# Delta-rule attention and two feed-forward layers on one core: another order of the blocks' stages

## The chip, the cores and the metric

One core of one Trainium2 chip runs the whole kernel. The metric is the device time of one execution in microseconds (us); the median of several runs counts. The engines are PE (matrix products), DVE, ACT and POOL (elementwise work) and SP, which issues all DMAs in program order. DVE, ACT and POOL each work through their instructions in the order in which the program issues them.

## The reference, cut to what matters

```python
for t in range(S):                       # B, H, S, D = 4, 8, 768, 48
    y[t] = q[t] @ state
    state += beta[t] * outer(k_n[t], v[t] - k_n[t] @ state)
x = y as [3072 tokens, 384]
h = x @ w_in;  x = (h * tanh(softplus(h))) @ w_out          # d_ff = 2048
P = exp(x @ w_gate - max);  8 rounds: P /= row sums; P /= column sums; P *= N / E
out = sum over e of P[:, e] * (relu(x @ w1[e]) @ w2[e])     # E = 8, F = 1024
```

## The kernel before, in words

The sequence is cut into 6 blocks of 128 positions, 512 tokens each over the 4 batches. Phase 1 goes through the blocks in 6 windows. Window c runs the first feed-forward layer on block c (16 groups of 128 hidden columns, loop L1267: `m_first`, `m_a`, `m_c`, `m_second`), then the hidden sums become the next input (`x2_done`, L993), and then expert 0 (8 groups, loop L1301: `e_first`, `e_relu`, `y0_second`). Every product is made of three passes with a high and a low part of each operand, since PE's fast number format is short. Phase 2 (L1362) does experts 1 to 7 in 168 pairs of (expert, block, group of 256 columns): `first` (L478) makes the products of seven-product form into four banks, `evacuate` (L503) turns them into the hidden values, `second` (L1335) multiplies by the second weight, a pair later.

Attention is hidden under phase 1. A block's *products* (`st_g`, L734) are the key-key and query-key products of 64 positions, copied out of PSUM, scaled and causally masked (`causal`, L706, on POOL). Then the triangular system of 32 x 32 pieces is eliminated on DVE: `lane_in_ops` (L768) transposes the pieces into a lane layout, `elim_ops` (L776) are 60 small operations, `st_lane_out` (L798) transposes back. The block's *chain* follows: `st_m1`, `st_place`, `st_m2` (L802 to L847) complete the inverse, and `st_z`, `st_w`, `st_s`, `st_y` (L852 to L914) carry the state through the block, each needing the one before. `st_x1` (L916) turns the tokens over for the first layer.

What sets the order is written out by hand. `window(c)` (L1188) puts stages at 28 marks (s0 to s15, f1 to f4, s16 to s23) according to the table `PLACES` (L1179): the chain of block c+1, and norms, loads and products of block c+2. `fill` (L1012) and `tick` (L590) take elimination operations from a queue `eq` at a given number of microseconds per group. The start-up (L1034 to L1165) does block 0's products, elimination and chain and block 1's products before window 0. While PE waits there, `warm` and `run_warm` (L1019 to L1031) issue products into a bank that nobody reads, the fillers. Part of block 1's elimination runs on POOL (`elim1`, L1120), the values are scaled on POOL (`prep_v`, L699).

The first layer's weights come as 64-bit numbers. `begin_decode` (ACT) and three DVE operations (`queue_decode`, L177) make 32-bit numbers of a chunk, `convert` (L231) splits it into high and low part (ACT, POOL), fetches a later chunk and stores the result to DRAM, from where later windows reload it (L242). The sums of expert 0 (`y0_done`, L952) and the hidden sums (`x2_done`, L1002) are copied into one tile `xr` and stored at once. `logits` (L1004) makes the gate's products of a block in one bank.

The eight rounds of column and row sums are a list of steps `sinks` (L370). `sink_step` takes one: two per group in window 5's last groups, then in phase 2 two after each `evacuate` and two after each `second`. In phase 2's first expert, x_begin/x_split/x_store (L452 to L469) make the split sums of the next block in four pairs; `acc_load` (L1366) loads expert 0's sums of a block, and when the rounds are done they are scaled by the gate, two tiles of 128 tokens per pair (L1401 to L1407).

Of the kernel before, what the change touches and what calls it, by code (L numbers as in the profile page):

```python
# [22 lines left out]
NTOK = B * S  # L23
# [61 lines left out]
def delta_mish_sinkhorn_kernel(  # L85
# [144 lines left out]

    def convert():  # L231
# [20 lines left out]
        if ch in w_dram:  # L252
            nc.sync.dma_start(out=w_dram[ch], in_=w.bitcast(F32))
        n = order_of[i] + 2
        if n < len(firsts):
            if kind(firsts[n]) == "plain":
                fetch(firsts[n])

# [100 lines left out]
    def sink_round_end():  # L359
# [3 lines left out]
        nc.vector.tensor_scalar(out=cr, in0=ps, scalar1=1e-9, scalar2=None, op0=ALU.add)  # L363
        nc.vector.reciprocal(out=cr, in_=cr)
        nc.vector.tensor_scalar(out=cr, in0=cr, scalar1=float(NTOK) / E, scalar2=None, op0=ALU.mult)
# [161 lines left out]
    if True:  # L527
# [173 lines left out]


# [65 lines left out]
        def lane_in_ops(c):  # L768
# [5 lines left out]
            )  # L774

# [167 lines left out]
        y0ps = {}  # L943

# [7 lines left out]
        def y0_done(c):  # L952
# [6 lines left out]
            nc.sync.dma_start(out=y0_dram[c], in_=y)  # L959
# [33 lines left out]
        def x2_done(c):  # L993
# [8 lines left out]
            nc.sync.dma_start(out=x2_dram[c], in_=xr)  # L1002

        def logits(c):  # L1004
            ps = bank()[:, 0:4 * E].rearrange("p (t e) -> p t e", e=E)
            for t in range(4):
                for k in range(KD):
                    mm(ps[:, t, :], lhsT=xr[:, k, t * 128:(t + 1) * 128], rhs=wg_sb[:, k, :], start=(k == 0), stop=(k == KD - 1))
            vec.tensor_copy(lg[:, 4 * c:4 * c + 4, :], ps)
# [24 lines left out]
        with tc.manual_schedule():  # L1034
# [8 lines left out]
            for t in range(4):  # L1043
                load_part(0, t, 1)
            for t in range(4):
                load_kq(1, t)
            load_vt(0)
# [28 lines left out]
            for _, op in lane_in_ops(0):  # L1076
                op()
# [6 lines left out]
            for t in range(4):  # L1084
                prep_ss(1, t)
            prep_root(1)
# [3 lines left out]
            for t in range(4):  # L1090
                run_warm(512, *[lambda hf=hf: st_g(1, t, hf, False) for hf in range(2)])
            el(12)
            for op in root_ops(1) + norm_ops(1, ALL):
                el(1)
                op()
            for t in range(4):
                prep_mb(1, t, nc.gpsimd)
            for t in range(2):
                mask_p(0, t)
            for t in range(2):  # L1100
                prep_v(0, t)
                first_r(0, t)
            for t in range(4):
                mask_g(1, t, nc.gpsimd)
            for t in range(2, 4):
                prep_v(0, t)
                mask_p(0, t)
            for n in range(3):
                begin_decode(n)
            el(len(e0) - 16)  # L1110
# [4 lines left out]
            in1 = deque(op for _, op in lane_in_ops(1))  # L1115
            in1.popleft()()
            elim_eng = [nc.gpsimd]
            ops1 = deque(op for _, op in elim_ops(1, elim_eng))

            def elim1(n, eng):  # L1120
                elim_eng[0] = eng
                for _ in range(min(n, len(ops1))):
                    ops1.popleft()()

            run_warm(2048, lambda: st_m1(0, 0), lambda: st_m1(0, 1))
            st_place(0, 0, (0, 2))
            while in1:
                in1.popleft()()
            run_warm(2048, lambda: st_m2(0, 0))

            def step(pool, decode, make, dve):
                elim1(pool, nc.gpsimd)
                decodes(decode)
                elim1(dve, nc.vector)
                converts(make)

            step(8, 1, 0, 0)
# [333 lines left out]
```

## Time and profile before

| | |
|---|---|
| median of 3 runs | 2372.87 us (2372.09 to 2378.44) |
| the profiled execution's own time | 2370.12 us |
| its span, first to last instruction | 2368.3 us |
| PE busy | 2254.5 us, 95% |
| DVE, ACT, POOL busy | 1236.1, 619.7, 529.4 us |
| DMA | 297 MB, 36% of 16 engines' span |

Times in rows are microseconds from the span's start unless ns stands with them. A row of a view of groups gives line, engine, operation, output and input names, shapes and count, then busy time and the mean of one in ns, then the idle time before them and what ended it. PE's clock is given as the granted share of 2.4 GHz: 1.0 is 2.4 and 0.5 is 1.2 GHz.

### The profile page before, as it was taken

The page shows a single profiled execution, that of the slowest core. Times are in us where ns is not written, and L with a number is a line of the kernel's source. Part 1 is how long each engine was busy: PE and PEld are TensorE (multiplying, and loading weights), DVE is VectorE, ACT ScalarE, POOL GpSimd, SP SyncE. Part 2 cuts the span into 40 slices and gives each one's busy share as a digit, 9 for nine tenths or more (in the row PEclk, how much of TensorE's full clock was granted, in tenths as well). Part 3 has the DMA queues.
Part 4 walks back from the last instruction along what each step waited for, and adds up shares of the span by engine and source line. Part 5 has one row for each costly group of instructions (what it writes and reads, how often), then busy time and mean ns, then how long its engine had stood idle before and what let it go on. Part 6 is the DMA issues. An engine that isn't in the chain of part 4 may idle for free.

```text
span 2368.3 us, 41965 instructions
## 1 busy us (share of the span) xinstructions
PE 2254.5 (95%) x18012; PEld 2084.9 (88%) x18012; DVE 1236.1 (52%) x2009; ACT 619.7 (26%) x1012; POOL 529.4 (22%) x439
## 2 busy tenths in 40 slices
PE   6698899999999999897999999999999999999998
PEld 3477778888888878897999999999999999999998
DVE  8875725427172123764555555555555555555554
ACT  5244332333323232221321221121122122112111
POOL 5586441331412051131300020030020002002000
PEclk7799999999999999998999999999999999999999
DMA  5367643637344565332231232222213113221321
GB/s 173 114 208 219 206 150 130 207 121 241 132 151 164 173 230 195 121 105 109 108 143 45 81 134 81 80 86 89 81 67 145 47 77 133 81 80 68 107 84 51
DMA packets 74441, 297.04 MB, mean 125 GB/s; under 512 B 7504, under 2 KB 39504, under 8 KB 68880
## 3 DMA queue, kind: packets, MB, share of 16 engines
q1 hardware_dynamic: 74256, 294.36, 36.0%
q8 instruction: 142, 2.33, 0.4%
q14 instruction: 43, 0.35, 0.0%
HBM read 247.15 MB, written 47.19 MB: 124 GB/s over the span
## 4 chain that ended last, share of the span: by engine, by line
issue 35%; PE 10%; DMA 5%; POOL 4%; DVE 1%; SPq 0%; ACT 0%; POOLq 0%; DVEq 0%; ACTq 0%
PE o L1348 5%; PE b L487 5%; DMA gr<-in_w_dram 4%; POOL gw L439 2%; POOL gx L439 1%; DMA acc<-y0d 1%; SPq L412 0%; POOL gx L466 0%; DVE acc L1353 0%; ACT gh L514 0%; DVE gt L510 0%; DVE gt L513 0%; ACT gw L437 0%; DVE gt L511 0%; DVE acc L1407 0%
## 5 line engine op out<-in xcount | busy, mean ns | idle before, releaser
L487 PE MATMUL b<-gx,gw 128*128 128x256 f32 x3564 | 452.5, 284 | 17.7 <-DVE gt L510 12.4
L487 PEld LDWEIGHTS b<-gx,gw 128*128 128x128 f32 x3564 | 444.2, 192 | 22.5 <-DVE gt L510 14.1
L1348 PE MATMUL o<-gw,gh 128*128 128x384 f32 x1728 | 443.0, 337 | 2.1 <-DVE acc L1353 2.1
L514 ACT ACTIVATE gh<-gt 128x1024 fp32r<-128x1024 f32 x168 | 178.3, 1061 | 647.2 <-DVE gt L513 647.2
L1348 PEld LDWEIGHTS o<-gw,gh 128*128 128x128 f32 x1728 | 309.7, 190 | 2.6 <-issue 2.6
L296 PE MATMUL psh<-xh,w 128*128 128x512 f32 x864 | 289.0, 416 | 23.2 <-DMA w<-wd 12.9
L515 DVE SCALAR_TENSOR_TENSOR gl<-gt,gh 128x1024 fp32r<-128x1024 f32 x168 | 209.6, 1247 | 189.4 <-ACT gh L514 189.4
L1348 PE MATMUL o<-gw,gl 128*128 128x384 f32 x864 | 291.1, 337 | 0.0
L510 DVE TENSOR_TENSOR gt<-b,gt 128x512 f32<-128x512 f32 x168 | 116.2, 691 | 302.0 <-PE b L487 238.1
L1348 PE MATMUL o<-gx,gh 128*128 128x384 f32 x960 | 247.5, 339 | 2.4 <-DVE acc L1353 2.4
L487 PE MATMUL b<-gx,gx 128*128 128x256 f32 x1980 | 243.7, 280 | 0.8 <-ACT gt L509 0.6
L487 PEld LDWEIGHTS b<-gx,gx 128*128 128x128 f32 x1980 | 240.4, 188 | 2.2 <-ACT gt L509 1.2
L296 PEld LDWEIGHTS psh<-xh,w 128*128 128x128 f32 x864 | 160.8, 195 | 65.1 <-issue 19.1
L978 POOL TENSOR_TENSOR gl<-x,gh 128x512 fp32r<-128x512 f32 x96 | 128.7, 1340 | 394.1 <-ACT gh L977 393.8
L439 POOL TENSOR_TENSOR gw<-gr,gw 128x512 fp32r<-128x512 f32 x72 | 90.8, 1293 | 561.4 <-ACT gw L437 561.4
L296 PE MATMUL psh<-xl,w 128*128 128x512 f32 x432 | 176.0, 407 | 4.2 <-DVE xl L607 4.2
L1348 PEld LDWEIGHTS o<-gx,gh 128*128 128x128 f32 x960 | 171.6, 188 | 2.9 <-issue 2.0
L1348 PEld LDWEIGHTS o<-gw,gl 128*128 128x128 f32 x864 | 163.6, 189 | 0.4
L1348 PE MATMUL o<-gx,gl 128*128 128x384 f32 x480 | 162.7, 339 | 0.0
L509 ACT ACTIVATE gt<-b 128x256 f32<-128x256 f32 x168 | 64.2, 382 | 352.2 <-PE b L487 328.9
L989 PE MATMUL x<-gh,w 128*128 128x512 f32 x576 | 150.0, 396 | 0.0
L439 POOL TENSOR_TENSOR gx<-gr,gx 128x512 fp32r<-128x512 f32 x40 | 50.4, 1294 | 440.9 <-ACT gx L437 440.9
(182 smaller groups left out, 2992.2 us busy)
## 6 DMA issues: line engine op xcount, KB each, us to landing
w<-wd SPq DMA_DIRECT2D x120, 768.0 KB, 4.6
gx<-xcd SPq DMA_DIRECT2D x36, 2304.0 KB, 9.0
gr<-in_w_dram SPq DMA_DIRECT2D x56, 384.0 KB, 3.6
wd<-w SPq DMA_DIRECT2D x24, 768.0 KB, 4.7
xcd<-gx SPq DMA_DIRECT2D x6, 2304.0 KB, 11.0
kq<-in_qkb_dram SPq DMA_DIRECT2D x20, 256.0 KB, 7.0
vt<-in_vtok_dram SPq DMA_DIRECT2D x6, 768.0 KB, 8.3
kq<-in_w_in_dram SPq DMA_DIRECT2D x12, 384.0 KB, 4.7
```

Of the source, the lines that this page charges most:

```text
L296: mm(ps, lhsT=wi(u, pw, kc), rhs=(xh, xl)[px][:, kc, :], start=(n == 0), stop=(n == 3 * KD - 1))
L439: nc.gpsimd.tensor_tensor(out=w[:, 1, q:q + 512], in0=r[:, q:q + 512], in1=w[:, 0, q:q + 512].bitcast(F32), op=ALU.subtract)
L487: mm(ps, lhsT=w[:, pw, a * 128:a * 128 + 128], rhs=x[:, px, b, :], start=(n == 0), stop=(n == last))
L509: nc.scalar.activation(out=t[:, 7], in_=b0[:, 0], func=AF.Copy)
L510: tt(out=t[:, 0:7:6], in0=b1, in1=t[:, 7:8].to_broadcast([128, 2, 256]), op=ALU.add)
L514: nc.scalar.activation(out=h, in_=t[:, 0:4], func=AF.Relu)
L515: nc.vector.scalar_tensor_tensor(out=l, in0=t[:, 0:4], scalar=0.0, in1=h.bitcast(F32), op0=ALU.max, op1=ALU.subtract)
L978: nc.gpsimd.tensor_tensor(out=l, in0=p, in1=h.bitcast(F32), op=ALU.subtract)
L989: mm(x2ps[c][k], lhsT=wo(u, pw, k * 128, k * 128 + 128), rhs=(h, l)[pg], start=(f == 0 and n == 0), stop=(f == U1 - 1 and n == 2))
L1348: mm(o[t], lhsT=(h, l)[ph][:, z, (t % 2) * 128:(t % 2) * 128 + 128], rhs=w[:, pw, at:at + DM], start=(g == 0 and fi == 0 and n == 0), stop ...
```

## The change

- Start-up: nearly all fillers go. Block 1's elimination leaves the start-up; `lane_in_one` and `elim_ops` of block 1 go into the queue `eq` for window 0. Its root goes from ACT and DVE to POOL's `prep_pow`, its norms and masks come later. The lane of blocks 0 and 1 is taken in by one transpose, after ACT copies (`diag_left`) and followed by POOL clearing (`diag_clear`). Block 0's values are scaled by 32 ACT operations (`prep_v_act`), its causal masks stand after the elimination in program order. Its value load is issued ahead of block 1's product operands. Four chunks instead of six are decoded before window 0, five and not six begun.
- `PLACES`: block 1's chain starts at mark 13 of window 0, two stages per mark, and block 2's products move from window 0 to marks 0 to 3 of window 1; block 3's products and block 2's chain are in window 1, block 4's with block 3's chain in window 2, and so on.
- Stores: a weight chunk's store is issued after the next chunk's fetch (`late_stores`); the stores of `xr` come three groups (expert 0's sums) or one group (hidden sums) later (`late_xr`).
- The gate's products are made in four parts, each copied out a mark later.
- In window 5 and in phase 2 the sum steps stand before the group's first products, two per pair (four in pair 0). Token sums are scaled four tiles per pair. `x_store(0)` goes from window 5 to pair 1, x_begin and x_split go one pair later. Two operations of a round's end become one.

The diff, cut:

```diff
@@ convert
-        if ch in w_dram:
-            nc.sync.dma_start(out=w_dram[ch], in_=w.bitcast(F32))
         n = order_of[i] + 2
         if n < len(firsts):
             if kind(firsts[n]) == "plain":
                 fetch(firsts[n])
+        flush_stores()
+        if ch in w_dram:
+            late_stores.append(lambda: nc.sync.dma_start(out=w_dram[ch], in_=w.bitcast(F32)))
@@ new
+        def prep_v_act(c, t):
+            ne = nrms[c % 2][1]
+            for h in range(H):
+                x = vt(c)[:, t, h * D:h * D + D]
+                nc.scalar.activation(out=x, in_=x, func=AF.Copy, scale=ne[:, t * H + h:t * H + h + 1])
+        def diag_left(c, t):
+            g = gx(c)[:, t]
+            for p in (32, 96):
+                nc.scalar.activation(out=g[p:p + 32, :, 0:32], in_=g[p:p + 32, :, 32:64], func=AF.Copy)
+        def lane_in_one(c):
+            v = gx(c).rearrange("p t h x -> p x (t h)")
+            return [
+                (1.94, lambda: nc.vector.transpose(out=lane, in_=v[:, 0:32, :])),
...
+                (0.0, lambda: diag_clear(c)),
@@ start-up
-            for _, op in lane_in_ops(0):
+                diag_left(0, t)
+            for _, op in lane_in_one(0):
                 op()
...
+                prep_v_act(0, t)
+            for t in range(4):
+                prep_ss(1, t)
+            prep_pow(1, ALL)
...
-            run_warm(2048, lambda: st_m1(0, 0), lambda: st_m1(0, 1))
+            work(1, 0)
+            run(lambda: st_m1(0, 0), lambda: st_m1(0, 1))
             st_place(0, 0, (0, 2))
...
+            for op in norm_ops(1, ALL):
+                op()
+            for t in range(4):
+                prep_mb(1, t, nc.gpsimd)
+            warm(1)
+            run(lambda: st_w(0, 0), lambda: st_w(0, 1))
+            work(2, 1)
...
+            for t in range(4):
+                diag_left(1, t)
+            eq.extend(lane_in_one(1) + elim_ops(1))
@@ PLACES
+            (13, two(17, 18, 20, 21, 22, 23, 24, 25), []),
+            (11, two(14, 15, 17, 18, 20, 21, 23, 24), [
+                (2, None, [-1, -1, 0, 1], two(0, 1, 2, 3), None, 3),
+                (3, 1, [14, 15, 17, 20], two(16, 19, 22, 25), 1, 25),
+            ]),
+            (5, spread(8, 23, 1, 16), [(4, 1, [9, 10, 12, 14], spread(11, 24, 1, 8), 1, 19)]),
+            (1, spread(4, 19, 1, 16), [(5, 1, [5, 6, 8, 10], spread(7, 19, 1, 8), 1, 19)]),
+            (0, spread(3, 19, 1, 16), []),
+            (0, [], []),
@@ windows
-                rate(0.4 if c == 0 else 0.6)
+                rate(0.6)
...
+                    if f == 4:
+                        flush_xr()
...
-                    fill(2.0)
+                    fill(2.0 if c else 1.7)
@@ phase 2
+                sink_step()
+                sink_step()
                 first(p)
                 evacuate(p)
-                sink_step()
-                sink_step()
+                if p == 0:
+                    sink_step()
+                    sink_step()
             if p >= 1:
                 second(p - 1)
-                sink_step()
-                sink_step()
...
+                if p == 1:
+                    x_store(0)
                 if e == 1 and i + 1 < NBLK:
-                    if g == 0:
+                    if g == 1:
                         x_begin(i + 1)
...
             if not sinks and todo:
-                for _ in range(2):
+                for _ in range(4):
```

## Rows read from the trace of the kernel before

**Rows 1.** Page: busy us, share of span and count; granted clock in 40 slices.

```profile
PE 2254.5 (95%) x18012; PEld 2084.9 (88%) x18012; DVE 1236.1 (52%) x2009; ACT 619.7 (26%) x1012; POOL 529.4 (22%) x439
...
PEclk7799999999999999998999999999999999999999
```

**Rows 2.** By stretch: length; busy PE, PEld, DVE, ACT, POOL; clock, DMA, GB/s.

```profile
0.00:113.81 113.81, 77.20 (x1126) 49.72 (x1126) 96.97 (x149) 44.36 (x133) 62.17 (x66) 0.73 0.45 138
113.81:275.19 161.38, 143.97 (x1441) 119.26 (x1441) 104.89 (x141) 66.71 (x110) 111.48 (x89) 0.93 0.66 218
275.19:425.41 150.22, 140.31 (x1392) 117.30 (x1389) 73.58 (x157) 44.23 (x82) 45.50 (x41) 0.94 0.48 159
425.41:565.34 139.93, 136.84 (x1392) 113.82 (x1390) 62.33 (x128) 43.78 (x82) 44.93 (x41) 0.99 0.53 172
565.34:704.00 138.66, 135.02 (x1392) 112.49 (x1390) 62.37 (x128) 43.79 (x82) 44.95 (x41) 1.00 0.49 162
704.00:830.48 126.48, 125.99 (x1200) 104.95 (x1198) 29.26 (x44) 36.36 (x62) 20.53 (x16) 1.00 0.48 163
830.48:950.19 119.71, 113.09 (x507) 93.85 (x505) 34.45 (x80) 39.02 (x61) 40.99 (x31) 0.94 0.54 205
```

**Rows 3.** Groups of DVE, 22 to 62.3: elimination of block 0.

```profile
L790 DVE TENSOR_TENSOR lane<-lane,t 128x30 f32<-128x30 f32 (+14 forms) x30 | 18.1, 603 | 0.9
L784 DVE TENSOR_TENSOR t<-lane 128x30 f32<-128x30 f32 (+14 forms) x30 | 18.0, 599 | 0.9
```

**Rows 4.** Groups of DVE, 660 to 800: elimination of a later block.

```profile
L790 DVE TENSOR_TENSOR lane<-lane,t 128x30 f32<-128x30 f32 (+14 forms) x30 | 10.0, 332 | 1.0
L784 DVE TENSOR_TENSOR t<-lane 128x30 f32<-128x30 f32 (+14 forms) x30 | 9.9, 331 | 0.9
```

**Rows 5.** Timeline of POOL: start us, us, operation, names, shapes, count, idle before.

```profile
35.34 5.58 POOL L709 TENSOR_TENSOR kq<-kq,mask_sb 64x512 f32<-64x512 f32 x4
...
221.24 5.45 POOL L656 TENSOR_TENSOR ne<-ss,half_sb 128x32 f32<-128x32 f32 x1 [6.87 <-DVE ss L640]
```

**Rows 6.** By stretch, columns as in rows 2: start-up, window 1, phase 2.

```profile
62.20:113.81 51.61, 37.63 (x694) 26.02 (x694) 45.74 (x55) 14.29 (x22) 31.81 (x35) 0.74 0.32 106
...
367.64:387.55 19.91, 17.35 (x231) 14.42 (x229) 9.47 (x15) 5.14 (x10) 5.89 (x7) 0.85 0.36 129
954.28:983.33 29.05, 22.55 (x124) 21.73 (x123) 21.06 (x50) 7.30 (x9) 8.66 (x6) 0.82 0.23 73
1067.41:1083.84 16.43, 9.83 (x58) 9.63 (x58) 9.32 (x19) 1.44 (x2) 0.00 (x0) 0.79 0.27 112
...
1083.84:1091.96 8.12, 8.12 (x59) 8.12 (x58) 5.18 (x9) 3.35 (x5) 2.15 (x1) 1.00 0.00 0
```

**Rows 7.** Timeline of DVE, start-up.

```profile
19.76 3.87 DVE L772 STREAM_TRANSPOSE lane<-gx 32x1024 f32<-32x1024 f32 x2
...
117.97 1.89 DVE L607 TENSOR_TENSOR xl<-psa,xh 128x512 fp32r<-128x512 f32 x3
```

**Rows 8.** Timeline of ACT, start-up.

```profile
13.68 0.24 ACT L650 ACTIVATE sq<-kt 128x48 f32<-128x48 f32 x1 [5.05 <-DMA kt<-in_ktok_dram]
...
13.92 0.23 ACT L650 ACTIVATE sq<-kt 128x48 f32<-128x48 f32 x1
...
22.69 4.86 ACT L704 ACTIVATE kq<-psa 64x512 f32<-64x512 f32 x8
...
37.44 0.76 ACT L704 ACTIVATE kq<-psa 64x256 f32<-64x256 f32 x2
...
113.16 1.57 ACT L922 ACTIVATE xh<-psa 128x512 fp32r<-128x512 f32 x3 [2.50 <-POOL w L249]
```

**Rows 9.** Timeline of PE, window 1.

```profile
296.71 1.19 PE L296 MATMUL psh<-xh,w 128*128 128x512 f32 x2 [6.84 <-DMA w<-wd]
```

**Rows 10.** Chain of waits, 1050 to 1085: start us, us, what.

```profile
1060.53 12.57 DMA acc<-y0d
```

**Rows 11.** Waits: engine and line, waited for: us in total, times, longest us.

```profile
DVE acc L1407 <- DMA acc<-y0d: 32.8, 3, 15.2
```

More of the change, by code (lines that the diff above doesn't have):

```diff
@@ L229, in drain_elim, with flush_stores @@
             eq.popleft()[1]()
+    late_stores = deque()
+    def flush_stores():
+        while late_stores:
+            late_stores.popleft()()
     def convert():
@@ L943, in delta_mish_sinkhorn_kernel, with flush_xr @@
         y0ps = {}
+        late_xr = deque()
+        def flush_xr():
+            while late_xr:
+                late_xr.popleft()()
         def y0_second(u):
@@ L1001, in x2_done, with logits, logits_out @@
                     nc.scalar.activation(out=xr[:, k, :], in_=x2ps[c][k], func=AF.Copy)
[L1002 to L1009, printed above, removed]
+            late_xr.append(lambda: nc.sync.dma_start(out=x2_dram[c], in_=xr))
+        lgps = []
+        def logits(c, t):
+            ps = bank()[:, 0:E]
+            for k in range(KD):
+                mm(ps, lhsT=xr[:, k, t * 128:(t + 1) * 128], rhs=wg_sb[:, k, :], start=(k == 0), stop=(k == KD - 1))
+            lgps.append((lg[:, 4 * c + t, :], ps))
+        def logits_out():
+            nc.vector.tensor_copy(*lgps.pop(0))
         def fill(us):
@@ L1143, in delta_mish_sinkhorn_kernel, with work @@
-            run_warm(1024, lambda: st_y(0, 0), lambda: st_y(0, 1))
+            for t in range(4):
+                mask_p(0, t)
+            def work(decode, make):
+                decodes(decode)
+                converts(make)
+            work(1, 0)
+            run(lambda: st_m1(0, 0), lambda: st_m1(0, 1))
+            st_place(0, 0, (0, 2))
+            run(lambda: st_m2(0, 0))
+            st_place(0, 1, (0, 2))
+            run(lambda: st_m2(0, 1))
+            for op in norm_ops(1, ALL):
+                op()
@@ L1150, in delta_mish_sinkhorn_kernel @@
-            run_warm(512, lambda: st_w(0, 2), lambda: st_w(0, 3))
-            begins(6)
-            step(2, 5, 3, 0)
-            run_warm(512, lambda: st_y(0, 2), lambda: st_y(0, 3))
+            converts(2)
+            warm(2)
+            run(lambda: st_z(0, 2), lambda: st_z(0, 3))
+            work(3, 2)
+            warm(1)
+            run(lambda: st_w(0, 2), lambda: st_w(0, 3))
+            for t in range(4):
+                mask_g(1, t, nc.gpsimd)
+            work(4, 3)
+            warm(1)
@@ L1154, in delta_mish_sinkhorn_kernel @@
+            run(lambda: st_y(0, 2), lambda: st_y(0, 3))
             for n in range(6, 8):
                 fetch(n)
-            step(4, 6, 5, 6)
             converts(4)
+            begins(5)
             early_ctx.close()
@@ L1165, in delta_mish_sinkhorn_kernel @@
             warm(2)
+            for t in range(4):
+                diag_left(1, t)
+            eq.extend(lane_in_one(1) + elim_ops(1))
         NU = U1 + U2
@@ L1192, in window @@
             late = {m: [] for m in MARKS}
-            nxt, far = c + 1, c + 2
-            rest[f"s{U1 + (c < NBLK - 1)}"].append(lambda: logits(c))
+            nxt = c + 1
+            for t in range(4):
+                k = MARKS.index(f"s{U1}") + (1 + t if c < NBLK - 1 else t // 2 - 1)
+                rest[MARKS[k]].append(lambda t=t: logits(c, t))
+                rest[MARKS[k + 1]].append(logits_out)
             if c == 0:
@@ L1275, in delta_mish_sinkhorn_kernel @@
                         m_c(b + f - 1)
-                    if not c and f < m0:
-                        elim1(10, nc.gpsimd)
                     if f == 0 and c:
```

146 lines of the change are left out of this document (61 added, 85 removed).

## The prediction, made before any run of the change

> **What bounds the kernel now.** I read the profile's page first: PE is busy 95% of the span, and the clock row is at its upper level except near the start and around the middle [rows 1]. So the time to win is where PE waits or runs at 1.2 GHz. The table by stretch [rows 2] cuts the span at the first weight product of each window of phase 1 and at the first one of phase 2. The start-up before window 0 takes 113.8 us at a mean clock of 0.73. Window 0 takes 161.4, window 1 150.2, window 2 139.9, window 3 138.7, window 4 126.5, window 5 up to phase 2 119.7. Windows 2 and 3 carry one block's chain and another block's products, window 4 a chain alone: a block's products cost some 12.2, the difference of windows 3 and 4. Against that, window 0 is about 23 too long and window 1 about 11.
>
> Inside the start-up the engine that decides is DVE. Its elimination of block 0 is 60 small operations. They take 0.60 us each there [rows 3], and 0.33 in a later block where POOL is quiet [rows 4]; 36.1 us against 19.9. POOL was at its causal masks meanwhile, 1.4 us each [rows 5]: a DVE operation with both operands in SBUF then lasts about as long as the POOL one. From 62.2 to 113.8 DVE is busy 45.7 of 51.6 [rows 6]. The first product of window 0 waits for the tokens' low part, which DVE ends at 119.9 [rows 7].
>
> **The change, part by part.** *Start-up, first half.* One transpose of 128 partitions takes in the lane, so two smaller ones, 3.87 together, go [rows 7]; ACT copies put ahead of it (two of 256 elements at 0.38 [rows 8] are on the path) cost 0.9 with their waits. Elimination starts 3 us earlier, at 20.8. With POOL quiet it takes 19.9 + 1.8 of idle [rows 4]. POOL's power of the norms now lands beside it: 5.45 [rows 5]. No row shows it beside a DVE operation on SBUF, so it costs between 0 and 5.45; I take 5, since the masks of the same engine did hold DVE up. The eight norm operations of block 1 leave this stretch. Elimination ends near 47.5, with two transposes of 2 us at 51.5; before it was 62.3 and 66.2.
>
> What is late next is ACT, which works in order. After its copies of the query products (end 27.5), it scales the values in 32 small operations (at most 0.24 each by the squares, which have a read-out between them [rows 8]; 0.19 taken, 6 us), then squares block 1 (32 at 0.24, 7.5), makes 24 copies of block 1's products at 0.38 (9.1), two negations (1) and four scalings of 768 (an estimate of 0.8 from 0.52 for 512, 3.2): 54.3. The first chain product's copies stand behind all this. So this point moves from 66.2 to 54.3: 12 us.
>
> *Start-up, second half.* From there to the end of the low parts it was 53.7. DVE loses a lane transpose set (5.9), 14 elimination operations of block 1 (4.6 at 0.33, 8.4 at 0.6; 7), and two of six decodes (six operations, some 1.4 each beside POOL; 8), and gains four norm operations (1). That is 20 off the engine that decides, for 34 us. POOL loses 18 or so elimination steps but gets block 1's masks, before the conversion that the token copies wait for [rows 8]; that is why I take no more. The low parts end near 88.5 and not 119.9, and the second group of window 0 starts 30.5 earlier. Bounds: 20, if ACT is 10 later than summed, to 36, if the power costs nothing.
>
> The fillers go with it. They ran in PE's waiting time, so I cost their removal at nothing; what it costs if they kept the clock up is next. With them the clock was still 0.73 in the mean before window 0 [rows 2]. The Trainium skill, page "TensorE: Matmul & The Clock Gate", section "Why this matters for your kernels", advises against idle gaps between bursts of products because the clock falls back. By that rule the chain's products would all run at the lower level. I estimate them at 20 of PE's 37.6 us from 62.2 on, the rest being fillers [rows 6]; from a mean clock of 0.74 to 0.5 they take 10 more. I keep the sum as it is, as DVE and ACT, not PE, end last there.
>
> *Window 0.* Block 2's products leave it: -12.2, with the wait for that block's loads, 0 to 6, taken as 5. DVE gets block 1's elimination in it: about 54 more operations and a transpose, while POOL has 89 instructions of 1.25 in the window [rows 2]. At 0.33 that is 18, partly in DVE's idle time (104.9 busy of 161.4); if every POOL instruction of the first 14 groups shut DVE out, it would be 25. I take 12, between the two. Sum -5.
>
> The Trainium skill, page "SBUF — State Buffer", section "Who interferes with whom", calls the port that DVE and GpSimd share an exclusive lock held for a whole instruction. By a strict reading window 0 would be 13 worse than summed; the rows show one DVE operation done per POOL mask, so not quite that. It is the first rival below.
>
> *Window 1* gets block 2's products: +12.2. The wait of 6.84 for a reloaded weight [rows 9] should go: SP issues in order, and the store of token sums, which waited for copies out of PSUM, no longer stands ahead of the reloads: -7. The chain no longer bunches in the group before the hidden sums, 19.9 long [rows 6], where two ordinary groups and the sums take about 13: -7. Sum -2.
>
> *Windows 2 to 4*: the stores' place, the gate logits in four pieces, and the norm's power away from a chain step; 0 to 4 each, taken as 5 in all. *Window 5*: the sums' products stand ahead of the weight products: -2. Late weight stores, one fused operation in each of eight rounds: nothing, DVE has room there. The first block's split sums are stored after pair 1, in a queue with room.
>
> *Phase 2.* The pairs from 954.3 to 983.3 take 29.05 where two take 2 x 8.12 [rows 6]: PE waits with the column sums' product, queued behind a pair. In the new order that product's input is made a pair earlier: -11, leaving 2. But the token sums are now scaled four per pair and not two. They catch up with their loads at the end of block 1 already, in pairs 7, 11 and 15. There DVE waits in order for a load that is 12.57 under way [rows 10], with the next evacuation behind it; before, it waited three times for 32.8 in all [rows 11], and two of them cost PE 16.4 - 8.1 = 8.3 each [rows 6]. A third such: +7. Sum -4.
>
> **The sum**: -30.5 - 5 - 2 - 5 - 2 - 4 = -48.5, on a profiled execution of 2370.1: 2321.6. The median of the runs is 2.75 above that execution, so I predict 2324.
>
> **The rivals.** *A. The shared port takes it back.* Block 1's elimination and the decodes meet all of POOL's work in window 0, and the masks meet the decodes in the start-up. Price: 25 instead of 12 there, 8 in the start-up: 2345. For it: DVE was busy 97 of 113.8 and slowed threefold [rows 2, 3]. Against: DVE idles a third of window 0. The Trainium skill's page "SBUF — State Buffer", in the section named above, has this as its rule.
>
> *B. Slower: the clock.* Without fillers PE enters window 0 at 1.2 GHz, and DVE's pace leaves a hole in each group, so the clock does not rise. Window 0's products, some 126 us at the upper level (as in window 4, which holds as much [rows 2]), would take up to 126 more; the holes of about 2 us in each of 24 groups, and DVE's share of the groups, hide half of that: 60 more, 2384. It decides from 48 us on, that is if more than three quarters of window 0 stay at the lower level. Against: window 0 had holes before and a mean clock of 0.93 [rows 2]. The Trainium skill's page "TensorE: Matmul & The Clock Gate", in the section named above, points this way.
>
> *C. Only the start-up counts.* The later windows keep their waits, because reloads are held by PE's use of the slots and not by SP: 7 in window 1, 5 in windows 2 to 4 and 2 in window 5 are lost: 2338.
>
> *D. The change does not do what it says*: ACT's 27 us of work before the first chain product grows, or a load of the first weights is late, so that the start-up gains 10 and not 30.5, and window 0 nothing: 2350.
>
> **How the numbers follow.** The forecast has 0.70, A 0.10, B 0.05, C 0.08, D 0.07. The forecast's own bounds (start-up 20 to 36, window 0 -18 to +8, the rest -22 to -5) reach from 2298 to 2345 with not all ends at once; A, C and D end at 2350, and 2356 allows for A with D in part. Range 2298 to 2356; left out are B, and a little on either side. A measurement of this kernel can tell about 0.3%, 7 us, from no change. Faster by more: the forecast, A and C, and nearly all of D, 0.93; within it 0.03; slower 0.04, most of B.
>
> **What would show it.** In the changed profile: elimination of block 0 at 0.33 to 0.45 per operation and done before 50; ACT without idle time from 20 to 54; the first weight product of window 0 near 87 and its group 4 to 5 long; window 0 about 150 to 155 with DVE and POOL both near full in its first half; window 1 near 148 without a wait for a reloaded weight; the first three pairs of phase 2 without the wait for the column sums; three waits of the evacuation for a token sum's load. The prediction is wrong if the weight products of window 0 start after 100, if window 0 takes over 170, or if the clock is under 0.8 in it.

## The result, and the profile after

The changed kernel takes 2402.43 us (median of 4 runs, 2397.57 to 2404.59), the kernel before on the same chip 2373.41: a ratio of 1.0115 [1.0094, 1.0137], so 27 us slower. Forecast were 2324 and a range up to 2356. The page, first the busy times and the clock, then the two groups of PE with the most idle time ahead of them:

```profile
PE 2261.3 (94%) x17981; PEld 2097.8 (87%) x17981; DVE 1255.1 (52%) x2057; ACT 632.8 (26%) x1059; POOL 500.1 (21%) x394
...
PEclk7898999999999999999999999999999999999999
...
L495 PE MATMUL b<-gx,gw 128*128 128x256 f32 x3564 | 460.3, 287 | 30.0 <-DVE gt L518 23.5
...
L305 PE MATMUL psh<-xh,w 128*128 128x512 f32 x864 | 290.4, 416 | 34.1 <-ACT x L1008 23.2
```

The same stretches as in [rows 2], with the same columns, cut at the first weight product of each window and of phase 2; the last row is phase 2 as a whole:

```profile
0.00:90.92 90.92, 70.40 (x1095) 50.94 (x1095) 66.40 (x126) 52.92 (x170) 43.02 (x34) 0.74 0.54 163
90.92:278.37 187.45, 147.56 (x1345) 118.91 (x1345) 127.67 (x163) 66.53 (x107) 89.19 (x58) 0.91 0.58 195
278.37:435.96 157.59, 146.26 (x1487) 123.31 (x1485) 86.45 (x162) 48.93 (x96) 58.97 (x59) 0.96 0.45 149
435.96:584.95 148.99, 138.48 (x1391) 115.63 (x1389) 79.80 (x171) 44.08 (x82) 45.02 (x41) 0.97 0.49 160
584.95:721.90 136.95, 134.54 (x1391) 112.39 (x1390) 61.56 (x131) 43.97 (x82) 44.75 (x41) 1.00 0.52 165
721.90:847.79 125.89, 125.66 (x1199) 104.83 (x1198) 29.45 (x47) 36.32 (x62) 20.54 (x16) 1.00 0.49 164
847.79:968.33 120.54, 112.65 (x506) 95.12 (x505) 30.49 (x71) 39.14 (x61) 40.86 (x31) 0.94 0.50 185
968.33:2402.80 1434.47, 1385.76 (x9587) 1376.68 (x9585) 773.29 (x1188) 300.89 (x402) 157.78 (x115) 0.99 0.26 93
```

Subtract [rows 2] line by line. The start-up is 22.9 shorter. Window 0 is 26.1 longer, window 1 7.4, window 2 9.1, window 5 0.8; windows 3 and 4 are 2.3 shorter. Phase 2 was 2368.30 - 950.19 = 1418.1 and is 16.4 longer. The sum is +34.5, the difference of the two spans. So the start-up gave nearly what it should, and window 0, windows 1 and 2, and phase 2 took it back with more.

**Window 0.** Counted from one group's first weight product to the next one's (s0 is the first group), s0 is 5.7 shorter than before, s3 to s13 are 9.7 longer (82.1 against 72.4), and s14 and s15, the last two groups before the hidden sums, are 22.0 longer (37.0 against 15.0). Expert 0's part is as long as it was, 58.0. In s14 and s15 block 1's `st_m1`, `st_m2` and the first stages of its chain now stand; before, then after, with the columns of [rows 2]:

```profile
202.21:217.20 14.99, 14.76 (x122) 11.92 (x118) 2.66 (x6) 6.27 (x12) 7.75 (x6) 1.00 0.82 257
183.38:220.40 37.02, 29.05 (x503) 24.30 (x502) 22.80 (x26) 16.95 (x28) 21.61 (x13) 0.80 0.57 168
```

PE has 503 products in them and not 122, and the clock is at 0.80 and not 1.00.

The groups before them show another cause. One of them, s6, 7.2 long where an undisturbed one takes 4.1, on DVE, then POOL, then ACT, then PE (timelines: start us, us, operation; in brackets the idle time before and its releaser):

```profile
122.63 1.94 DVE L816 TENSOR_TENSOR t<-lane 128x238 f32<-128x238 f32 x1
124.49 1.64 DVE L185 TENSOR_SCALAR kq<-kq 128x768 int32<-128x768 int32 x1
126.23 1.40 DVE L188 SCALAR_TENSOR_TENSOR kq<-kq 128x768 int32<-128x768 int32 x1
127.66 0.96 DVE L193 SCALAR_TENSOR_TENSOR kq<-kq 128x768 int32<-128x768 int32 x1
```

```profile
122.42 1.88 POOL L257 TENSOR_TENSOR w<-kq,w 128x768 fp32r<-128x768 f32 x1 [3.48 <-ACT w L256]
124.39 1.30 POOL L1015 TENSOR_TENSOR gl<-x,gh 128x512 fp32r<-128x512 f32 x1
125.67 1.14 POOL L703 TENSOR_TENSOR vt<-vt,ne 128x384 f32<-128x384 f32 x1
```

```profile
128.65 0.92 ACT L256 ACTIVATE w<-kq 128x768 fp32r<-128x768 f32 x1 [4.39 <-DVE kq L193]
...
130.26 0.58 ACT L1008 ACTIVATE x<-psh 128x512 f32<-128x512 f32 x1
```

```profile
130.89 0.50 PE L305 MATMUL psh<-xh,w 128*128 128x512 f32 x1 [1.03 <-ACT x L1008]
```

Read it from the end. PE waits for the activation L1008 to empty a bank. ACT works in order and has that activation behind the conversion L256, which waited 4.39 for DVE's decode. DVE had the decode behind elimination operations. And each DVE operation that meets one of POOL's three instructions ends shortly after that one does, 0.27, 0.44 and 0.82 later: L816, 0.41 where POOL is quiet (experiment 1), lasts 1.94 beside the 1.88 of L257. The wait of 1.03 is a third of the 3.1 that this group is too long. Most of the rest is the clock: after the wait ahead of the group, 1.93, it is at 0.57 in the group's first 4 us, and the nine weight products take 3.98 where those of s3 took 2.04 at 1.00:

```profile
123.65:127.63 3.98, 3.90 (x9) 2.81 (x10) 3.87 (x3) 0.61 (x1) 3.06 (x3) 0.57 0.53 126
```

DVE has no room left in these groups; the stretch from 101 to 185.5, columns as above:

```profile
101.32:185.50 84.18, 58.64 (x207) 42.06 (x206) 81.08 (x92) 30.02 (x43) 49.08 (x31) 0.92 0.58 192
```

**Phase 2.** In pair 0, whose first products begin at 968.33, PE stands 6.4 ahead of a sum's product, and DVE's timeline says why: evacuation first (971.46 to 976.3), then a whole round (from L372 on):

```profile
979.05 0.57 PE L370 MATMUL psa<-gate 128*128 128x8 f32 x2 [6.39 <-DVE gate L366]
```

```profile
971.46 0.68 DVE L518 TENSOR_TENSOR gt<-b,gt 128x512 f32<-128x512 f32 x1
...
976.25 0.16 DVE L372 TENSOR_SCALAR gate<-psa 128x8 f32<-128x8 f32 x1
...
978.41 0.49 DVE L366 TENSOR_REDUCE gate<-lg 128x8 f32<-128x192 f32 x1
```

By pairs, after less before: pairs 0 to 4 are +7.0, -5.2, -5.1, +1.2, +3.3 (+1.2 together), pair 9 is +9.1, and pairs 13 and 17 are +2.4 and +3.5. Pair 9 is the new wait for a token sum's load, its row first, then the waits for these loads, which were 32.8 [rows 11]:

```profile
1054.43:1071.61 17.18, 10.12 (x59) 9.91 (x58) 9.36 (x17) 2.36 (x3) 0.00 (x0) 0.80 0.23 98
```

```profile
DVE acc L1463 <- DMA acc<-y0d: 47.2, 3, 16.3
```

### The profile page after: what moved, and what is told of

The parts are those of the page before. It is cut to its first block, busy times and chain, and to the rows that moved or that the text cites. A ratio compares the mean times of both kernels' runs of the same rounds, so it can differ in the third digit from the quotient of the medians.

```text
span 2402.8 us, 41937 instructions
## 1 busy us (share of the span) xinstructions
PE 2261.3 (94%) x17981; PEld 2097.8 (87%) x17981; DVE 1255.1 (52%) x2057; ACT 632.8 (26%) x1059; POOL 500.1 (21%) x394
## 4 chain that ended last, share of the span: by engine, by line
issue 28%; PE 18%; DMA 4%; POOL 4%; SPq 0%; DVE 0%; ACT 0%; POOLq 0%; DVEq 0%; ACTq 0%
PE o L1399 9%; PE b L495 9%; DMA gr<-in_w_dram 3%; POOL gw L447 2%; POOL gx L447 1%; DMA acc<-y0d 1%; POOL gx L474 0%; SPq L420 0%; DVE acc L1404 0%; DVE acc L1463 0%; DVE gt L518 0%; ACT gx L473 0%; DVE gt L521 0%; ACT gx L445 0%; ACT gh L522 0%
## 5 line engine op out<-in xcount | busy, mean ns | idle before, releaser
L495 PE MATMUL b<-gx,gw 128*128 128x256 f32 x3564 | 460.3, 287 | 30.0 <-DVE gt L518 23.5
L495 PEld LDWEIGHTS b<-gx,gw 128*128 128x128 f32 x3564 | 451.6, 196 | 35.1 <-DVE gt L518 25.5
L305 PE MATMUL psh<-xh,w 128*128 128x512 f32 x864 | 290.4, 416 | 34.1 <-ACT x L1008 23.2
## 6 DMA issues: line engine op xcount, KB each, us to landing
xcd<-gx SPq DMA_DIRECT2D x6, 2304.0 KB, 11.1
```

The lines of the kernel that those rows point to most:

```text
L305: mm(ps, lhsT=wi(u, pw, kc), rhs=(xh, xl)[px][:, kc, :], start=(n == 0), stop=(n == 3 * KD - 1))
L495: mm(ps, lhsT=w[:, pw, a * 128:a * 128 + 128], rhs=x[:, px, b, :], start=(n == 0), stop=(n == last))
```

## The experiments

Ratios are to the kernel before on the same chip; a difference of 0.001 is 2.4 us. Profiled executions of kernels with the same lines differ: the start-up of the changed kernel, kept unchanged in eight others, ended between 84.8 and 90.9 (mean of the nine 87.0), and window 1 with the same lines took 157 to 165, at mean clocks from 0.96 down to 0.90. A single stretch is therefore read to some 5 us.

**1. Low parts of window 0 on DVE.**

```diff
-        nc.gpsimd.tensor_tensor(out=w[:, 1], in0=r, ...)
+        (nc.vector if kind(i) == "wide" and i >= 4 else nc.gpsimd).tensor_tensor(out=w[:, 1], in0=r, ...)
-            nc.gpsimd.tensor_tensor(out=l, in0=p, ...)
+            (nc.vector if u < U1 else nc.gpsimd).tensor_tensor(out=l, in0=p, ...)
```

> The changed kernel, with the low parts of window 0 (the 12 weight chunks from the fifth on and the 16 groups' hidden values) subtracted on DVE in place of POOL. Theory P (the port): in window 0 DVE has no idle time in groups 3 to 13, and of its 7 us per group some 2.7 are spent waiting beside POOL's two subtractions (1.9 and 1.3 us). Moved to DVE they cost it about 1.0 and 0.7 but free it of those 2.7: groups of about 5.8 and not 7.2, window 0 about 14 shorter (187 to about 173), the run near 2388. Rival W (the amount of work: DVE simply has too many operations there): DVE gets 1.7 more per group, window 0 is some 18 longer, the run near 2420. Rival L (the loop decode, conversion, activation between DVE, ACT and POOL sets the pace through its waits, not the time of any engine): within 5 of the changed kernel.

Measured: 2389.49, ratio 1.0060 [1.0041, 1.0080], 13 less than the changed kernel; window 0 is 172.36. From first weight product to first weight product, groups s6 to s13 last 5.5 in the mean and not 7.5, though s3 and s4 wait longer (14.8 and 9.5). DVE by operation and shape, first the changed kernel in 101 to 178, then this one in 120 to 170:

```profile
L188 DVE SCALAR_TENSOR_TENSOR kq<-kq 128x768 int32<-128x768 int32 x11 | 16.5, 1497 | 1.1
L185 DVE TENSOR_SCALAR kq<-kq 128x768 int32<-128x768 int32 x11 | 13.9, 1265 | 0.0
...
L816 DVE TENSOR_TENSOR t<-lane 128x240 f32<-128x240 f32 x2 | 2.4, 1178 | 0.1
```

```profile
L188 DVE SCALAR_TENSOR_TENSOR kq<-kq 128x768 int32<-128x768 int32 x9 | 8.6, 959 | 0.3
...
L257 DVE TENSOR_TENSOR w<-kq,w 128x768 fp32r<-128x768 f32 x9 | 8.6, 951 | 0.0
L1015 DVE TENSOR_TENSOR gl<-x,gh 128x512 fp32r<-128x512 f32 x10 | 6.8, 684 | 0.0
L185 DVE TENSOR_SCALAR kq<-kq 128x768 int32<-128x768 int32 x9 | 5.0, 555 | 0.0
L816 DVE TENSOR_TENSOR t<-lane 128x240 f32<-128x240 f32 x2 | 0.8, 408 | 0.1
```

With two more DVE operations per group, 1.6 of work, the groups got 2.0 shorter: the same decode step takes 0.96 and not 1.50, the shift 0.56 and not 1.27, an elimination step 0.41 and not 1.18. That is theory P; W, more work on DVE, has the wrong sign.

**2. No elimination of block 1.**

```diff
-            eq.extend(lane_in_one(1) + elim_ops(1))
+            eq.extend(lane_in_one(1))
```

> The changed kernel without the 60 elimination operations of block 1 in window 0 (they are left out of the computation). Theory D (DVE's time bounds groups 3 to 13, elimination is the part that came new): groups fall from 7.2 to about 5.2, window 0 from 187 to about 163, and the wait of 3.2 for the lane transposes goes: the run near 2378. Rival L (the loop between the decode, the conversion on ACT and the activation sets the pace): groups stay near 7, the run near 2400. Rival E (window 0 was lengthened by the bunched chain steps in expert 0's part and not by elimination): first part unchanged, no more than 5 gained.

Measured: 2383.60, ratio 1.0036 [1.0023, 1.0048], 19 less. Groups s4 to s9 fell to 5.0 to 5.7. The first part of window 0, up to the hidden sums, is the first row below; it is 129.48 in the changed kernel and was 217.20 - 113.81 = 103.4 before:

```profile
84.83:195.97 111.14, 89.89 (x800) 70.00 (x800) 91.70 (x69) 54.84 (x86) 81.70 (x46) 0.92 0.67 221
```

So in window 0 elimination costs 18, and 8 of the 26 remain without it. Theory D for the groups s3 to s13, which fall from 82.1 to 60.9; but s14 and s15 stay long (39.9, against 15.0 before), so the bunched chain that rival E named costs too, ahead of expert 0's part. The elimination takes DVE 37.5 us in this part of the changed kernel, and without it DVE's busy time falls by 17.7 alone (109.36 to 91.70): the 36 decode operations that now meet POOL's instructions take 67.8 and not 47.9.

**3. Two token-sum tiles per pair** (`range(4)` back to `range(2)`; some tiles are then scaled after expert 1's part has been added to them).

> The changed kernel with two token-sum tiles scaled per pair and not four. Theory T (four per pair catch up with the loads at the end of block 1 and make a third wait, and make the other two longer): the pair of 17.2 goes back to about 8.1, the two of 18.9 and 19.4 to about 16.4 and 15.9, so 12 to 15 less: the run near 2389. Rival Q (the wait comes from the load itself, which stands behind other transfers in SP's queue after the new order of the token splits): the third wait stays, 0 to 3 less, the run near 2401.

Measured: 2395.24, ratio 1.0083 [1.0061, 1.0106], 8 less. The third wait goes, pair 9 is again at 8.1. Pairs 13 and 17 stay at 18.0 and 19.1: theory T for the third wait, not for the other two.

**4. No extra sum steps in pair 0** (the two `sink_step()` behind `evacuate` go; block 0's first addition then uses the factors of the round before the last).

> The changed kernel without the two sum steps that pair 0 of phase 2 takes behind its evacuation. Theory S (the second round of pair 0 puts its column sums' product on PE behind an evacuation and a round on DVE, a hole of 6.6): pair 0 goes from 11.1 to about 5, pair 1 stays near 10 or falls to 9, a round moves one pair later at no cost: 5 to 7 less, the run near 2396. Rival R (the round only moves and costs the same in the pair where it lands): 0 to 2 less, the run near 2401.

Measured: 2404.62, ratio 1.0122 [1.0099, 1.0145]. Pair 0 falls from 11.1 to 4.2, but pairs 2, 4, 8 and 9 take 12.4, 14.2, 16.4 and 14.5 where they took 8.4, 11.8, 10.8 and 17.2. Rival R: a round that stands ahead of an evacuation costs its time in whichever pair it lands.

**5. Late stores alone, on the kernel before** (`late_stores`, `flush_stores`, `late_xr`, `flush_xr` of the diff and nothing else).

> The kernel before with the late stores alone (a weight chunk's store behind the next chunk's fetch, the stores of sums three groups or one group later). Theory Q (SP's order held the reload): the wait of 6.84 for a reloaded weight in window 1's fourth group goes, window 1 falls from 150 to about 143, and windows 2 and 3 lose 0 to 2 each: the run near 2365. Rival H (the reload is held by PE's use of the slot or by the load itself): the group stays at 11, the run near 2373.

Measured: 2361.39, ratio 0.9941 [0.9921, 0.9960]: **14 less than before**. The group of the reload takes 4.1 and not 11.1, and window 1:

```profile
273.05:413.88 140.83, 137.43 (x1391) 115.41 (x1390) 72.85 (x157) 44.23 (x82) 45.36 (x41) 0.98 0.51 169
```

Theory Q: SP's order held the reload. Window 1 gained 9.4; the start-up 2.7, which is within its spread.

**6. The first half of the start-up alone, on the kernel before.** As in the change: `diag_left`, `lane_in_one`, `prep_v_act`, `prep_pow(1)`, masks of block 0 behind the elimination; block 1's norms after 24 elimination operations.

```diff
-            el(12)
-            for op in root_ops(1) + norm_ops(1, ALL):
+            el(24)
+            for op in norm_ops(1, ALL):
                 el(1)
                 op()
```

> The kernel before with the first half of the start-up alone: one transpose into the lane behind ACT copies, block 0's values scaled on ACT, block 1's power of the norms on POOL, block 0's causal masks behind the elimination. Block 1's elimination stays in the start-up, partly on POOL, and window 0 and the fillers stay. Theory F (the elimination of block 0 beside POOL's masks costs what it lost, and the gain is kept): elimination ends 8 to 12 earlier, window 0 starts near 103 and not 114, its length stays near 161: the run near 2362. Rival G (the second half is bound by DVE beside POOL, which now has the masks there): the start of window 0 moves by less than 4, the run near 2371.

Measured: 2388.84, ratio 1.0058 [1.0032, 1.0084]: slower by 14. Neither theory. This row of DVE has the reason:

```profile
50.59 0.18 DVE L678 TENSOR_SCALAR ne<-ne 128x32 f32<-128x32 f32 x1 [19.48 <-POOL ne L656]
```

DVE stood 19.5 in the midst of the elimination, because the norms stood there in its order and waited for POOL's power, which waited for ACT's 32 squares behind 32 scalings. The changed kernel has those norms behind the elimination.

**7. Block 2's products back in window 0, chains as before.** (Part of block 2's products is scaled with a later tile's factors here.)

```diff
-            (13, two(17, 18, 20, 21, 22, 23, 24, 25), []),
-            (11, two(14, 15, 17, 18, 20, 21, 23, 24), [...]),
-            (5, spread(8, 23, 1, 16), [(4, 1, [9, 10, 12, 14], spread(11, 24, 1, 8), 1, 19)]),
+            (13, two(17, 18, 20, 21, 22, 23, 24, 25), [(2, None, [19, 20, 21, 22], two(21, 22, 23, 24), None, 24)]),
+            (3, spread(6, 19, 1, 16), [(3, 3, [6, 7, 9, 11], spread(8, 19, 1, 8), 1, 19)]),
+            (0, spread(3, 19, 1, 16), [(4, 1, [4, 5, 7, 9], spread(6, 19, 1, 8), 1, 19)]),
```

> The changed kernel with block 2's products back in window 0 (two at a time at marks 21 to 24) and the chains and products of windows 1 to 3 at the marks of the kernel before; block 1's chain stays in expert 0's part of window 0. Theory B (the length of windows 1 and 2 comes from the chain and products that the moved block 2 pushes into expert 0's part): window 1 falls from 157.6 to about 143 (150 of before less the reload wait of 7), window 2 from 149 to about 140; window 0 grows by 5 to 12 as the products come on top of the chain: the run between 2382 and 2393. Rival N (the windows are long for another reason, such as the stores or the gate's parts): windows 1 and 2 stay within 4 of the changed kernel, the run near 2410.

Measured: 2395.57, ratio 1.0088 [1.0059, 1.0117], 6 less. The two parts of window 0, then window 1 and window 2:

```profile
87.59:215.59 128.00, 95.66 (x800) 72.48 (x800) 110.82 (x129) 54.55 (x86) 73.22 (x46) 0.89 0.58 189
215.59:293.64 78.05, 65.65 (x643) 57.18 (x641) 38.42 (x81) 17.27 (x34) 29.53 (x30) 0.85 0.40 148
293.64:431.73 138.09, 135.42 (x1391) 114.10 (x1390) 71.15 (x155) 44.23 (x82) 45.06 (x41) 0.99 0.52 172
431.73:571.76 140.03, 136.50 (x1392) 113.55 (x1390) 62.44 (x131) 43.89 (x82) 44.98 (x41) 0.99 0.52 172
```

Window 1 falls by 19.5 and window 2 by 9.0, as theory B has it. Window 0 grows by 18.6, all of it in its second part (57.97 in the changed kernel), more than the 5 to 12 expected: among the bunched stages of block 1's chain, block 2's products cost 20 (with the start of its elimination), not the 12.2 that windows 3 and 4 show for a spread chain. The 19.5 of window 1 is not their price there. In the changed kernel they stand at marks 0 to 3, ahead of the chain, and these four groups take 20.9 against 14.5 here. Most of the 19.5 is expert 0's part, 52.9 against 35.2, where the changed kernel has block 2's chain two stages at a time and block 3's products.

**8. Window 1's chain spread** (block 2's elimination at 3.4 and not 2.0 per group, chain from mark 9, `spread(12, 27, 1, 16)`).

> The changed kernel with block 2's elimination at 3.4 per group of window 1 and not 2.0, so that its chain starts at mark 9 and not 11 and goes one stage per mark from 12 to 27. Theory U (two chain stages per mark, each needing the one before, leave PE waiting in groups 12 to 22): those groups lose some 10 of their 27 of waits, window 1 falls from 157.6 to about 148: the run near 2393. Rival V (what waits in these groups is the products' copies and masks on ACT and POOL, or DVE's late elimination): window 1 within 3 of 157.6, the run near 2402.

Measured: 2406.63, ratio 1.0129 [1.0092, 1.0165]; window 1 is 162.1. Theory U falls: the earlier start only moved the wait for the lane transposes (a group of 18.3), and expert 0's part stayed at 54.8 against 52.9. What does wait there (rival V) is not shown by this run.

**9. Late stores and the start-up's first half, mended:** block 1's norms and masks behind `st_lane_out(0)`.

> The kernel before with the late stores (2361 in the run of these alone) and the first half of the start-up, now with block 1's norms, masks and causal masks all behind block 0's elimination, so that DVE's order has nothing in it that waits for ACT's squares. Theory F: elimination of block 0 ends near 44 as in the changed kernel, window 0 starts 8 to 14 earlier than 111: the run near 2350. Rival G (some 21 of POOL's masks now stand ahead of block 1's lane and elimination, and the second half takes the gain back): window 0 starts at 105 to 113, the run near 2360.

Measured: 2358.07, ratio 0.9934 [0.9910, 0.9958]. Block 0's elimination ends at 43.6, but window 0 starts at 106.95. The stretch from 62 to it:

```profile
62.00:106.95 44.95, 32.06 (x490) 22.49 (x490) 41.23 (x50) 9.67 (x14) 38.87 (x41) 0.70 0.35 123
```

DVE is busy 41 of 45 and POOL 39: rival G. The first half's gain of some 18 shrinks to 4 to 7 while the rest of the work stays in the second half. It is the fastest kernel of the study, level with experiment 5 within their intervals, and both beat the kernel before and the changed one.

**10. Phase 2 and window 5 of before in the changed kernel** (sum steps behind `evacuate` and `second`, `range(2)`, splits a pair earlier, `x_store(0)` in window 5).

> The changed kernel with window 5's and phase 2's order of the kernel before: sum steps behind the evacuation and behind the second product, two token-sum tiles per pair, the token splits a pair earlier, the first block's split sums stored in window 5. Theory T: all of the 16 that phase 2 got longer come from these few lines, pairs 0 to 17 take again what they took before: the run near 2387. Rival C (they are longer because what the changed windows left open, such as stores and loads in SP's queue, ends there): 0 to 6 less, the run near 2399.

Measured: 2389.57, ratio 1.0069 [1.0044, 1.0095], 11 less. Phase 2, from its first product to the end, against 1434.47:

```profile
961.72:2382.60 1420.88, 1382.55 (x9585) 1373.74 (x9584) 771.30 (x1180) 301.18 (x402) 158.85 (x115) 0.99 0.26 92
```

Theory T for 13.6 of the 16.4. Pairs 13 and 17 stay at 18.1 and 19.0 with the old lines too, 4.7 over before, so that part is not of this order; in experiment 9 the same two were within 0.3 of the kernel before. Over all profiles the two together take 32.2 to 34.1 in the five kernels with the start-up's second half and the marks of the kernel before, and 35.1 to 38.3 in the nine with the changed start-up, whichever order phase 2 has. So this part, some 4, comes with the changed phase 1, as rival C has it; by which of its lines, no run shows.

**11. Late stores and the low parts of window 0 on DVE, on the kernel before** (the edit of experiment 1, weight chunks from the seventh on).

> The kernel before with the late stores and with window 0's low parts (hidden values, and weight chunks from the seventh on) subtracted on DVE in place of POOL. By the port (theory P), POOL's instructions in window 0 fall by 26 and each had held DVE up by more than DVE takes for it; but in this kernel PE is full in most groups of window 0, so the groups with waits (the sixth to the ninth) lose 4 to 8 in all: the run near 2356. Rival W (DVE's added work stands ahead of the elimination and chain copies): window 0 grows by 5, the run near 2366.

Measured: 2363.62, ratio 0.9966 [0.9947, 0.9984]; window 0 is 160.76 against 161.89 with the late stores alone. Nearer to W's number, but the window did not grow, and the 4 to 8 of theory P did not come either. PE is busy 144 of the 161, so there was little for a freer DVE to give; that this is the reason is argued, not shown.

**12. The changed kernel with experiments 1, 7 and 10 together** (block 2's scaling tiles one mark later than in 7).

> The changed kernel with all three returned: low parts of window 0 on DVE, block 2's products in window 0 at marks 21 to 24 with the chains of windows 1 to 3 as before, phase 2 and window 5 as before. Theory S (the losses are three separate ones and add): 2402 less 13, 7 and 16 is 2366, window 0 near 190, window 1 near 138, phase 2 as before. Rival I (they overlap: what is won in window 0 is waited for again in its last groups): 2375 to 2385.

Measured: 2369.27, ratio 0.9995 [0.9978, 1.0013]. The ratio falls by 0.0120, 28 us; the three alone gave 0.0055, 0.0027 and 0.0046, 30 in sum. Window 0 is 195.2 (190 expected), window 1 145.8 (138) and phase 2 1419.3 (1434.5 in the changed kernel, 1418.1 before). Theory S: within the intervals the three losses are separate and add.

It also shows what the start-up's gain was worth. With the same products in it again, window 0 ends at 280.15 here, at 275.19 in the kernel before and at 273.05 with the late stores alone. So the 26 or more by which it starts earlier are paid again inside it, by the work that moved there, and this kernel stays 13 behind experiment 5, whose late stores it has too (0.9995 against 0.9941).

## Why the prediction was wrong

*Start-up (-30.5).* Right in mechanism and nearly in size: elimination of block 0 in the changed kernel is 60 operations at the pace of [rows 4],

```profile
L822 DVE TENSOR_TENSOR lane<-lane,t 128x30 f32<-128x30 f32 (+14 forms) x30 | 10.0, 333 | 1.0
L816 DVE TENSOR_TENSOR t<-lane 128x30 f32<-128x30 f32 (+14 forms) x30 | 9.9, 331 | 1.1
```

and ends at 43.9, where I had 47.5: POOL's power of the norms (5.43 from 43.62) came at the end, beside two transposes of 2.04 and 1.89 that it did not stretch, so the 5 that I took for it was 0. (In window 2 it stands beside eleven operations of another elimination and does not stretch these either; see the last section.) ACT's copies for the first chain product start at 56.0 (54.3 summed). Window 0 starts 22.9 earlier in this execution; by the means of the executions, 87.0 against 113.3 (113.8, 111.2 and 115.0 with before's start-up), it is 26. The prediction counted to window 0's second group: that starts at 95.0 and not 123.6, 28.6 earlier, and 32 by the means (91.1 against 123.3). Experiment 9, which has the first half without the second, gains 4 to 7: the rest hangs on what left the second half, block 1's elimination and two decodes. But all of it was moved and not saved (experiment 12).

*Window 0 (-5): the step that failed.* Counted from its second group, as the prediction does, it went from 151.6 to 183.4: +31.8. Two terms were wrong. First, the elimination that comes in: I took 12 of DVE's time "between the two" bounds of 18 and 25, below both, because DVE idled a third of the window before. But that idle time lay elsewhere. Before the change DVE idled 56.5 of the window, 4.7 of it in the first of these two stretches, in the midst of the loop, and 26.7 in the second, around the hidden sums:

```profile
160.00:205.00 45.00, 43.75 (x568) 36.24 (x565) 40.29 (x45) 20.05 (x29) 30.39 (x17) 0.96 0.67 219
205.00:240.00 35.00, 28.81 (x214) 23.42 (x214) 8.34 (x19) 14.05 (x27) 21.89 (x16) 0.83 0.78 224
```

In the changed kernel DVE is full in the groups where elimination stands (81.1 of 84.2 us from 101.3 to 185.5), and through ACT's order its delays reach PE. It cost 18 (experiment 2). I had read the row of one operation per POOL instruction [rows 3, 5], and did not carry it to window 0, where POOL is busy 49.1 of the same 84.2. Second, I costed block 1's chain, moved to marks 17 to 25 two stages at a time, at nothing. It made s14 and s15 22.0 longer, and experiment 2 leaves these two groups long. In expert 0's part experiment 7 shows that block 2's products are worth 20, and yet it takes 57.97 after and 275.19 - 217.20 = 58.0 before: the moved chain used up what the products left. So the -12.2 and -5 credited there were not to be had. No run moves this chain alone; its price is read from these rows.

A smaller term was left out: the two decodes credited with 8 in the start-up come back in window 0, where 36 decode operations stand and not 30, and I charged nothing for them there. No run prices them alone.

*Rival A* named the mechanism, with 25 for elimination and 8 in the start-up; its 2345 lacks the chain, the later windows and phase 2. (Its "slowed threefold" is 1.8-fold by [rows 3] and [rows 4].) The Trainium skill, page "SBUF — State Buffer", section "Who interferes with whom", states that a DVE operation with two SBUF inputs contends with a POOL instruction that reads SBUF. Experiment 1's rows agree: 1178 against 408 ns for the same step. I had called it "not quite that" and gave it a tenth. The power of the norms does not fit that sentence: it reads SBUF and held up no operation with two inputs (last section), so here the measurement decides. The page also exempts an operation with one SBUF input outside the two-port modes; two transposes beside a mask and two subtractions of POOL (2.10 and 1.97, at 186.5 and 188.5) agree. The single-input shift (1265 against 555 ns) does not, unless it ran in such a mode. That it takes 555 ns alone, where operations with two inputs of the same 128x768 take 951 and 959, speaks for one; no run tests it.

*Rival B*, the clock, did not happen in its size: 0.91 in window 0 against 0.93, without the fillers. By these means PE had 34 us at 1.2 GHz there and not 23, which I estimate at up to 6 us of the loss. *C* was wrong in its reason: reloads were held by SP (experiment 5). *D* was not the case.

*Window 1 (-2; it was +7.4).* The reload wait went as summed, 7 to 9. The relief of the chain's bunch did not come: the group before the hidden sums takes 23.4 where it took 19.9. The products at marks 0 to 3 cost little, 6.4 by experiment 7; what I had at nothing was block 2's chain, bunched again with block 3's products in expert 0's part, which takes 52.9 where it took 37.9.

*Windows 2 to 4 (-5; +6.8).* I saw the stores and not that block 3's chain now stands at marks 8 to 23 where it stood at 3 to 18, and block 4's products with it. With the old marks window 2 is 140.0 again. Windows 3 and 4 together are 2.3 shorter, which is within what a stretch can tell.

*Phase 2 (-4; +16.4).* The third wait of +7 was right (+9.1). The sums' -11 was wrong: a round takes DVE some 2.6 (976.25 to 978.9), and ahead of the first products it stands before the evacuation in DVE's order, so it is paid for again in each pair; pair 0 with two rounds pays 7. Pairs 0 to 4 came out even (+1.2), and experiment 4 shows the cost moving with the round. The rest, some 6 in pairs 13 and 17, I did not foresee; 4.7 of it came with the changed phase 1 (experiment 10), by what stays open.

Of what would show it wrong, "window 0 over 170" was the sign that came.

## What to carry to other kernels

Price work that moves to an engine by that engine's time in the very groups it enters, beside the other engine's instructions there, and not by its idle share of a whole window. A dependent chain that is moved is a cost of its own, at its new place: two stages at a time it made two groups 22 longer, and a block's products put among such stages cost 20 where they cost 12 among a spread chain. Check a stage that got shorter together with the stage that took its work: here both together gained nothing. Take a bundled change apart: the one part of this bundle that needed nothing else, the late stores, gives 0.6% by itself, and the rest undid it.

## What was unexpected of the hardware

Not every POOL instruction holds DVE up. In window 2 of the changed kernel the power of the norms, which has both inputs in SBUF, lasts 5.51, and eleven two-input operations of block 3's elimination stand beside it and keep their pace of 0.32 to 0.39 each; the shape 128x210 takes 0.38 here and 0.38 in the start-up with POOL quiet. POOL's row, then that of DVE:

```profile
448.14 5.51 POOL L664 TENSOR_TENSOR ne<-ss,half_sb 128x32 f32<-128x32 f32 x1 [3.00 <-DVE ss L648]
```

```profile
448.81 0.38 DVE L816 TENSOR_TENSOR t<-lane 128x210 f32<-128x210 f32 x1
```

The shift of 128x768 took 0.55 beside another power (at 47.64), where beside POOL's subtractions it took a mean of 1.27. So the price of a POOL instruction to DVE is not its length: the power, which I had priced at up to 5.45, cost nothing. It works on 32 elements per partition, the subtractions, masks and scalings that held DVE up on 384 to 768; what makes the difference no run tests.

And the same instructions at the start of the program took 84.9 in one execution (experiment 10) and 90.9 in another (the changed kernel), at mean clocks of 0.82 and 0.74.
